# Running a filter's preparation in the unit that takes it, and three smaller reorderings, in a Fourier filter plus mixture-of-experts kernel

## The chip, the cores and the metric

The kernel runs on one core of one Trainium2 chip. The time is the device time of one execution in microseconds (us). Engines: PE (matmuls; PEld is its weight loads), DVE (vector), ACT (scalar), POOL (GpSimd), SP (issues nearly all DMAs). Each works through a queue of its own in order, and waits on semaphores.

## The reference, cut to what matters

```
xn  = layernorm(x)                                    # 2048 x 512
A   = irfft2(rfft2(xn) * (w_r + 1j * w_i))            # the filter
B   = sum over 8 experts e: gate_e(xn) * (gelu(xn @ w1[e]) @ w2[e])   # F = 1792, all experts kept
out = x + A + B
```

## The kernel before, in words

The experts' hidden columns are cut into 56 chunks of 256. Two are done in a front part (to about 133 us); the other 54 are taken in 27 pairs `c`, each for two halves `i` of the rows: 54 **units** `u = 2c + i`. `i = 0` is called a first half, `i = 1` a second half. Both layers of a unit are block products with fewer multiplications than the plain ones (Strassen-Winograd), so a unit has 7 products for layer 2 of the unit before and 7 for its own layer 1 (14 in all, 12 matmuls of 128x512 each). The PE order of a unit, by the tiles' names (weights `ua`, `us` and inputs `xr` for layer 1, `va`, `vs` and `hs` for layer 2; PSUM banks `A`, `B`, `C`):

`a11` to B, [layer 2] `s4` to C, `a12` to B, [layer 2] `s3` with input T3 to C, `s2` to A, [layer 2] `a11` to B, `s1` to A, [layer 2] `a12` to B, `s4` to A, [layer 2] `s1` with T1 to C, `s3` to B, [layer 2] `a22` with T4 to C, `a22` to B, [layer 2] `s2` with T2 to A.

The layer 2 products add up in place: after each, DVE adds the bank to the result (`acc<-C,acc`, `acc<-B,acc`, `acc<-A,acc`) before the next product may go on in that bank. The inputs of layer 2 are split in a rounded high part (ACT, `CAST hs<-c`) and the rest, the low part (DVE or POOL, `TENSOR_TENSOR hs<-c,hs`); a product reads the low part in its last four matmuls only.

`layer1` is a generator of 21 steps, `layer2` one of 7; the loop `for n in range(7)` at the end of `body` runs three steps of `layer1` (`one`) and one of `layer2` (`second`) per round, and puts the filter in between. The filter is a list of `chunks`, each a pair (PE part, DVE and ACT part, cost); `slot_pe()` issues the PE part of the next chunk and puts its other part into `todo`; `slot_dve()` issues what is in `todo`. All these are put in each engine's queue in the order of the code (`pin`); only the DMAs' places on SP are found when the program is built.

The filter has two kinds of chunks, for even and then odd frequencies. **Table chunks** (19 for each of four transforms; here "table" chunks have a PE part) issue 6 or 12 small matmuls into `psf` that need what the chunk before prepared: DVE `us<-us`, `B<-psf,B` or `C<-psf,C`, `uz<-us,uz` and ACT copies (line 438 is the filter's `op`). **Radix chunks** have no PE part: `radix4` (10 chunks of one `step` each, the last four half as large), `twiddle`, `multiply`, `combine`, `save`, `restore`; they are DVE operations on `Y` and the tiles `A` to `D`.

Before the change a unit takes table chunks in rounds 0, 2, 3 and 5, and radix chunks in rounds 0, 2, 3, 4 and, in first halves, 5. What was taken in round 5 is issued on DVE in round 0 of the next unit (`kept_back`), and what was then taken in round 0 only at the end of round 1.

Of the kernel before, what the change touches and what calls it, by code (L numbers as in the profile page):

```python
# [91 lines left out]
def r32(ap):  # L92
    return ap.bitcast(F32)
# [26 lines left out]
def body(ctx: ExitStack, tc: tile.TileContext, io):  # L120
    plain_order, strict, pinned = False, False, {}

    def pin(ins):
        if strict:
            engine = ins.ins.engine
            last = pinned.get(engine)
            if last is ins.ins:
                return ins
            if last is not None:
                tc.add_manual_dep(  # L130
                    ins.ins, last.name,
                    mybir.DependencyInfo(mybir.DependencyClass.NoSync, mybir.DependencyReason.DATA), reason="layout",
                )
            pinned[engine] = ins.ins
        return ins
# [51 lines left out]
    def load(src):  # L187
        raw = keep.tile([P, 8 * FC], F32, name="raw")
        nc.sync.dma_start(raw, src)
        return raw  # L190
# [46 lines left out]
    def move(dst, src):  # L237

        with tc.issue_after(last_sp[0]) if last_sp[0] else nullcontext():
            last_sp[0] = nc.sync.dma_start(dst, src).ins  # L240
# [185 lines left out]
    def filtered(p):  # L426
# [5 lines left out]
        out, of = [], {}  # L432

        def chunk(dve, cost, pe=None):
            out.append((pe, dve, cost))

        def op(fn, *args, **kw):
            return pin(fn(*args, **kw))  # L438
# [86 lines left out]
        def radix4(inner, sgn, first=None):  # L525

            def y(i):
                return of["Y"][:, i : i + 13 : 4] if inner else of["Y"][:, 4 * i : 4 * i + 4]

            def step(n):  # L530
                if n == 0 and first:
                    first()
                y0, y1, y2, y3 = (y(i) for i in range(4))
                t1, t3 = of["T1"], of["T3"]
                if n < 6:
                    add, d, a, b = (
                        (0, t1, y0, y2), (1, y0, y0, y2), (0, t3, y1, y3), (1, y1, y1, y3), (0, y2, y0, y1), (1, y0, y0, y1)
                    )[n]
                    op(V.tensor_add if add else V.tensor_sub, d, a, b)
                    return  # L540
                d, sg = ((y1, sgn), (y3, -sgn))[(n - 6) // 2]
                c = n % 2
                op(V.tensor_sub if (sg > 0) != c else V.tensor_add, d[:, :, c], t1[:, :, c], t3[:, :, 1 - c])

            for n in range(10):
                chunk(lambda n=n: step(n), 1.3 if n < 6 else 0.8)

        def twiddle(sgn):

# [45 lines left out]
        ends = slice(0, P + 1, P)  # L595

        def save():
            rev, w, z, ta, tb = (of["ends"][:, n] for n in range(5))
            op(V.tensor_add, w[:, :, 0], w[:, :, 0], rev[:, :, 0])
            op(V.tensor_sub, w[:, :, 1], w[:, :, 1], rev[:, :, 1])  # L600
            op(V.tensor_copy, z, of["Y"][:, :, :, ends])
            op(V.tensor_mul, ta, z, w[:, :, :1].to_broadcast([P, NB, 2, 2]))
            op(V.tensor_mul, tb, z, w[:, :, 1:].to_broadcast([P, NB, 2, 2]))

        def restore():
            rev, w, z, ta, tb = (of["ends"][:, n] for n in range(5))
            Y = of["Y"]
            op(V.tensor_sub, Y[:, :, 0, ends], ta[:, :, 0], tb[:, :, 1])
            op(V.tensor_add, Y[:, :, 1, ends], tb[:, :, 0], ta[:, :, 1])
            op(V.tensor_sub, Y[:, :, 0, :1], Y[:, :, 0, :1], Y[:, :, 1, P : P + 1])  # L610
            op(V.tensor_add, Y[:, :, 1, :1], Y[:, :, 1, :1], Y[:, :, 0, P : P + 1])

        if p == 0:
            chunk(save, 1.0)
        for j in range(8):
            chunk(lambda j=j: multiply(j), 1.4)
            chunk(lambda j=j: combine(j), 1.0)
        if p == 0:
            chunk(restore, 0.8)
        radix4(True, 1, narrow)  # L620
        twiddle(1)
        radix4(False, 1)
# [223 lines left out]
    chunks = deque()  # L846
# [7 lines left out]
    todo = []  # L854
# [18 lines left out]
    def slot_dve():  # L873

        while todo:
            todo.pop(0)()
# [83 lines left out]
    def xin(n, i):  # L960
        if (n, i) in ahead:
            return ahead.pop((n, i))
        x = xr.tile([P, 2, 2, TB], F32R, name="xr", bufs=3)
        last_x[0] = nc.sync.dma_start(r32(x), xs[n][i]).ins
        return x
# [333 lines left out]
    second, old, rs, spots = iter(()), [], {}, []  # L1299
    strict = True  # L1300
    for u in range(2 * N2):
        c, i = divmod(u, 2)
        if u and i == 0:
            raw = load(io["wb"][c])
            step2 = prepare(rp, "v", sums2(raw), w2q)
        if u == 1:
            ahead.update({(n, 1): xin(n, 1) for n in ("b11",)})
            behind = last_x[0]
            with tc.issue_after(behind):
                for b in range(NB - 4, NB):  # L1310
                    nc.sync.dma_start(res[b], acc[:, b, :])
            acc = keep.tile([P, 4, 2, 2, TB], F32, name="acc")
            ahead.update({(n, 1): xin(n, 1) for n in ("b21", "T1")})
            with tc.issue_after(last_x[0]):
                for n in ("T2", "T4"):
                    move(xs[n][1], r32(ahead[n, 1]))
        if i == 1 and c + 1 < N2:
            with tc.issue_after(behind) if u == 1 else nullcontext():
                raw = load(io["wa"][c + 1])
            step1 = prepare(wq, "u", sums1(raw, False), w1q)  # L1320
        hs = {}
        one = layer1(c, i, dict(w1q), hs, old)

        def weights(n):
            nonlocal strict
            strict = u > 0
            for _ in range(((3, 1, 1, 1, 1, 0, 0), (0, 0, 0, 2, 2, 2, 1), (0, 1, 1, 1, 2, 2, 1), (0, 1, 1, 1, 1, 2, 1))[min(u, 2 + i)][n]):
                with tc.issue_after(last_act[0]) if u == 0 else nullcontext():
                    next(step1 if i else step2, None)
            strict = True  # L1330

        end = u + 1 == 2 * N2
        if end:
            assert not chunks
            raw2 = raw[:, 2 * F2 : 3 * F2]
            nc.sync.dma_start(raw2, io["wb"][c][:, 2 * F2 : 3 * F2])
            y = ft.tile([P, NB, 2, P + 1], F32R, name="Y").rearrange("p a b c -> p (a b c)")
            both = [
                y[:, k * 4 * D : (k + 1) * 4 * D].rearrange("p (h k d) -> p h k d", h=2, k=2) for k in range(2)
            ]  # L1340
            ident = ft.tile([P, 2, 2, P], F32R, name="uz")
            ident = r32(ident.rearrange("p a b c -> p (a b c)"))[:, :P]
            nc.sync.dma_start(ident, idd)
            for n in "ABCD":
                y = wide(n)
                spots += [y[:, k * D : (k + 1) * D] for k in range(2)]
        for n in range(7):
            next(one)
            kept_back = bool(todo)
            if n == 0:  # L1350
                slot_dve()
            if u and not end and chunks:
                short = chunks[0][2] < 1.35 and not chunks[0][0]
                if n == 2 or n == 0 and u > 1 or n == 4 and short or n == 5 and (chunks[0][0] or i == 0 and short):
                    slot_pe()
            if n == 0 and not kept_back:
                slot_dve()
            if i:
                weights(n)
            if u == 1 and n == 0:  # L1360
                next(second)
            next(one)
            if u != 1 or n:
                next(second, None)
            if u and n == 3 and not end:
                slot_pe()
            if n in (2, 3, 4):
                slot_dve()
            next(one)
            if n == 1:  # L1370
                slot_dve()
            if not i:
                weights(n)
            if end:
                if n == 0:
                    finals(1)
                if n == 2:
                    split(both[0][:, :, :, FC:], raw2.rearrange("p (k f) -> p k f", k=2), nc.gpsimd)
                if 3 <= n < 6:
                    name = ("a11", "a12", "a22")[n - 3]  # L1380
                    dh, fh = (int(digit) - 1 for digit in name[1:])
                    pin(nc.scalar.copy(both[fh][:, :, :, dh * FC : (dh + 1) * FC], r32(w2q[name])))
                for b in ((), (), (12, 13), (14, 15), (4, 5), (6,), (7,))[n]:
                    rs[b] = rows_of(b, 1)
        second = layer2(c, i, w2q, hs)
# [53 lines left out]
```

## Time and profile before

| | us |
|---|---|
| median of 3 runs (lowest, highest) | 2479.45 (2474.74, 2481.25) |
| profiled execution | 2478.03 |
| its span, first to last instruction | 2476.2 |
| PE busy | 2342.3 (95%) |
| DVE busy | 1947.1 (79%) |
| POOL busy | 1411.9 (57%) |
| ACT busy | 1126.0 (45%) |

The profile is one execution. A row of the timeline gives start, duration, engine, line, operation, tiles, shapes and, in brackets, how long the engine had been idle and what ended that. L105 is the helper through which all main instructions go, L438 the filter's. Windows are given in us from the span's start; "PEclk" is the granted TensorE clock as a share of full speed. The units lie from 133.2 us (`u = 1`) to 2446 us; the table chunks fall in units 2 to 6, 22 to 31 and 48 to 52, the radix chunks in between.

### The profile page before, as it was taken

The page shows a single profiled execution, that of the slowest core. Times are in us where ns is not written, and L with a number is a line of the kernel's source. Part 1 is how long each engine was busy: PE and PEld are TensorE (multiplying, and loading weights), DVE is VectorE, ACT ScalarE, POOL GpSimd, SP SyncE. Part 2 cuts the span into 40 slices and gives each one's busy share as a digit, 9 for nine tenths or more (in the row PEclk, how much of TensorE's full clock was granted, in tenths as well). Part 3 has the DMA queues.
Part 4 walks back from the last instruction along what each step waited for, and adds up shares of the span by engine and source line. Part 5 has one row for each costly group of instructions (what it writes and reads, how often), then busy time and mean ns, then how long its engine had stood idle before and what let it go on. Part 6 is the DMA issues. An engine that isn't in the chain of part 4 may idle for free.

```text
span 2476.2 us, 27849 instructions
## 1 busy us (share of the span) xinstructions
PE 2342.3 (95%) x10478; PEld 1925.2 (78%) x10478; DVE 1947.1 (79%) x1753; ACT 1126.0 (45%) x1559; POOL 1411.9 (57%) x790
## 2 busy tenths in 40 slices
PE   9998889999999999998899889999999999989899
PEld 7777777778887778777787777778877787777777
DVE  8665666999889989867676667999889989866676
ACT  6554444454444454434344444454444454443342
POOL 3364445667666766654364445776666766653553
PEclk9999999999999999999999999999999999999999
DMA  7886756666677676767676556666666666766673
GB/s 255 321 310 220 235 198 230 238 237 239 240 258 268 213 280 219 263 240 257 225 246 221 200 215 212 236 228 240 230 246 211 247 219 232 266 236 240 235 258 139
DMA packets 123718, 588.58 MB, mean 238 GB/s; under 512 B 13600, under 2 KB 16288, under 8 KB 66880
## 3 DMA queue, kind: packets, MB, share of 16 engines
q1 hardware_dynamic: 122784, 574.06, 65.6%
q10 hardware_dynamic: 800, 12.74, 1.3%
q8 instruction: 83, 1.36, 0.2%
q14 instruction: 51, 0.42, 0.1%
HBM read 550.96 MB, written 48.37 MB: 242 GB/s over the span
## 4 chain that ended last, share of the span: by engine, by line
PE 77%; DVE 17%; ACT 2%; issue 2%; DMA 2%; POOL 0%; SPq 0%; ACTq 0%; DVEq 0%; POOLq 0%
PE B L105 31%; PE C L105 20%; PE A L105 19%; DVE c L105 7%; PE psf L438 5%; DVE acc L105 3%; DVE hs L105 2%; PE p L105 2%; DVE Y L438 2%; ACT hs L105 1%; DVE us L438 1%; PE psf L105 1%; DMA hs<-xs_T 1%; DVE uz L438 1%; DVE xr L105 1%
## 5 line engine op out<-in xcount | busy, mean ns | idle before, releaser
L105 POOL TENSOR_TENSOR hs<-c,hs 128x1024 fp32r<-128x1024 f32 x161 | 428.1, 2659 | 408.3 <-ACT hs L105 404.1
L105 ACT CAST hs<-c 128x1024 fp32r<-128x1024 f32 x375 | 390.4, 1051 | 217.6 <-DVE c L105 123.3
L105 PE MATMUL C<-hs,vs 128*128 128x512 f32 x1884 | 472.2, 401 | 8.7 <-DVE acc L105 8.7
L105 PE MATMUL A<-xr,us 128*128 128x512 f32 x1920 | 463.2, 390 | 0.0
L105 PE MATMUL B<-xr,ua 128*128 128x512 f32 x1884 | 455.5, 391 | 0.0
L105 PEld LDWEIGHTS C<-hs,vs 128*128 128x128 f32 x1884 | 365.2, 195 | 89.7 <-ACT ua L105 8.2
L105 PEld LDWEIGHTS A<-xr,us 128*128 128x128 f32 x1920 | 359.9, 188 | 74.8
L105 PEld LDWEIGHTS B<-xr,ua 128*128 128x128 f32 x1884 | 353.5, 188 | 76.3 <-DVE c L105 1.8
L105 DVE TENSOR_TENSOR hs<-c,hs 128x1024 fp32r<-128x1024 f32 x214 | 337.4, 1593 | 31.5 <-ACT hs L105 31.5
L105 DVE TENSOR_TENSOR c<-c 128x1024 f32<-128x1024 f32 x212 | 326.3, 1539 | 0.1
L105 PE MATMUL B<-hs,va 128*128 128x512 f32 x1248 | 312.3, 400 | 13.9 <-DVE acc L105 13.0
L105 DVE TENSOR_TENSOR acc<-C,acc 128x1024 f32<-128x1024 f32 x207 | 251.7, 1216 | 90.0 <-PE C L105 90.0
L105 PEld LDWEIGHTS B<-hs,va 128*128 128x128 f32 x1248 | 239.3, 194 | 70.2 <-DVE acc L105 17.2
L105 DVE TENSOR_TENSOR acc<-B,acc 128x1024 f32<-128x1024 f32 x103 | 125.7, 1220 | 156.0 <-PE B L105 156.0
L105 POOL TENSOR_TENSOR ua<-raw,ua 128x512 fp32r<-128x512 f32 x81 | 123.5, 1524 | 186.2 <-ACT ua L105 168.4
L105 ACT ACTIVATE c<-c 128x1024 f32<-128x1024 f32 x108 | 114.8, 1063 | 251.2 <-DVE c L105 251.2
L105 POOL TENSOR_TENSOR va<-raw,va 128x512 fp32r<-128x512 f32 x81 | 145.9, 1802 | 106.7 <-ACT va L105 106.7
L105 DVE TENSOR_TENSOR c<-c,cwb 128x1024 f32<-128x1024 f32 x108 | 196.8, 1822 | 1.5 <-ACT c L105 1.5
L105 ACT COPY c<-A 128x1024 f32<-128x1024 f32 x108 | 109.6, 1015 | 184.1 <-PE A L105 153.5
L105 DVE TENSOR_TENSOR c<-B,c 128x1024 f32<-128x1024 f32 x107 | 130.7, 1221 | 72.6 <-PE B L105 68.7
L105 PE MATMUL C<-hs,va 128*128 128x512 f32 x660 | 160.0, 391 | 0.2
L105 PE MATMUL B<-xr,us 128*128 128x512 f32 x636 | 153.4, 390 | 0.0
(188 smaller groups left out, 3071.6 us busy)
## 6 DMA issues: line engine op xcount, KB each, us to landing
xr<-xs_T SPq DMA_DIRECT2D x212, 1024.0 KB, 5.1
xr<-xs_b SPq DMA_DIRECT2D x161, 1024.0 KB, 5.1
cwb<-cwd SPq DMA_DIRECT2D x124, 256.0 KB, 5.0
raw<-in_wa SPq DMA_DIRECT2D x27, 1024.0 KB, 4.9
raw<-in_wb SPq DMA_DIRECT2D x27, 1024.0 KB, 4.9
xs_T<-Y SPq DMA_DIRECT2D x8, 1024.0 KB, 6.1
us<-xfd SPq DMA_DIRECT2D x32, 256.0 KB, 4.5
D<-mbd SPq DMA_DIRECT2D x32, 256.0 KB, 4.1
```

The source lines that it names most:

```text
L105: return lambda *args, **kw: self.order(made(*args, **kw))
L438: return pin(fn(*args, **kw))
```

## The change

1. A table chunk's DVE and ACT part is issued in the unit that took it: the one of round 5 in round 5, after the gate's multiplication of `h22`; the one of round 0 in round 0, after the low part of T3.
2. The fifth radix chunk of first halves is taken in round 1 and issued after T4's difference (`less(o12, o22, o21)`), not in round 5 and issued at the start of the second half.
3. Layer 2's first product and its `acc<-C,acc` come ahead of T3's low part on DVE.
4. The four half-size steps of each `radix4` become two chunks of two; `save` and `restore` become two chunks each. No operation is added or taken away; the filter has 14 chunks less (200, not 214).

```
-            for n in range(10):
-                chunk(lambda n=n: step(n), 1.3 if n < 6 else 0.8)
+            for n in range(6):
+                chunk(lambda n=n: step(n), 1.3)
+            for n in (6, 8):
+                chunk(lambda n=n: (step(n), step(n + 1)), 1.3)
...
         if p == 0:
-            chunk(save, 1.0)
+            chunk(save, 1.4)
+            chunk(save2, 1.4)
...
         if p == 0:
-            chunk(restore, 0.8)
+            chunk(restore, 1.4)
+            chunk(restore2, 1.3)
...
         for n in range(7):
             next(one)
-            kept_back = bool(todo)
-            if n == 0:
-                slot_dve()
             if u and not end and chunks:
-                short = chunks[0][2] < 1.35 and not chunks[0][0]
-                if n == 2 or n == 0 and u > 1 or n == 4 and short or n == 5 and (chunks[0][0] or i == 0 and short):
+                table = bool(chunks[0][0])
+                short = not table and chunks[0][2] < 1.35
+                if n == 2 or n == 0 and u > 1 or n == 4 and short or n == 5 and table or n == 1 and i == 0 and short:
                     slot_pe()
-            if n == 0 and not kept_back:
+            if n == 0 and todo and not table:
                 slot_dve()
             if i:
                 weights(n)
-            if u == 1 and n == 0:
-                next(second)
+            if n == 0:
+                next(second, None)
             next(one)
-            if u != 1 or n:
+            if n in (0, 5):
+                slot_dve()
+            if n:
                 next(second, None)
             if u and n == 3 and not end:
                 slot_pe()
             if n in (2, 3, 4):
                 slot_dve()
             next(one)
             if n == 1:
                 slot_dve()
```

**DVE at the seam of two table units** (end of `u = 3`, start of `u = 4`), from the gate's multiplication of `h22` on. `C<-psf,C` belongs to the chunk taken in round 5; `acc<-A,acc` ends the old unit's products, the last `hs<-c,hs` is T3's low part. Before:

```order
L105 TENSOR_TENSOR c<-c,cwb 128x1024
L105 TENSOR_TENSOR acc<-C,acc 128x1024
L105 TENSOR_TENSOR c<-B,c 128x1024
L105 TENSOR_TENSOR hs<-c,hs 128x1024
L105 TENSOR_TENSOR acc<-A,acc 128x1024
L105 TENSOR_TENSOR c<-c 128x1024
L438 TENSOR_TENSOR us<-us 128x256
L438 TENSOR_TENSOR C<-psf,C 128x260
L438 TENSOR_TENSOR uz<-us,uz 128x256
L105 TENSOR_TENSOR hs<-c,hs 128x1024
L105 TENSOR_TENSOR acc<-C,acc 128x1024
L105 TENSOR_TENSOR c<-c,cwb 128x1024
```

The same stretch now:

```order
L105 TENSOR_TENSOR c<-c,cwb 128x1024
L438 TENSOR_TENSOR us<-us 128x256
L438 TENSOR_TENSOR C<-psf,C 128x260
L438 TENSOR_TENSOR uz<-us,uz 128x256
L105 TENSOR_TENSOR acc<-C,acc 128x1024
L105 TENSOR_TENSOR c<-B,c 128x1024
L105 TENSOR_TENSOR hs<-c,hs 128x1024
L105 TENSOR_TENSOR acc<-A,acc 128x1024
L105 TENSOR_TENSOR c<-c 128x1024
L105 TENSOR_TENSOR acc<-C,acc 128x1024
L105 TENSOR_TENSOR hs<-c,hs 128x1024
L438 TENSOR_TENSOR us<-us 128x256
```

The three filter operations moved up by five operations; T3's low part stands behind `acc<-C,acc`; and the next chunk's `us<-us`, which stood behind T4's difference, six operations after T3's low part, follows that part at once.

**SP in a second half with table chunks** (`u = 5`), `xs_b_113` being the input of `a11` and `xs_T_115` that of `s2`. Before:

```order
L964 DMA xr<-xs_b_113 128x2048
L400 DMA cwb<-cwd 128x512 x2
L964 DMA xr<-xs_b_117 128x2048
L189 DMA raw<-in_wa 128x2048
L964 DMA xr<-xs_T_115 128x2048
L964 DMA xr<-xs_T_121 128x2048
L240 DMA us<-xfd_111 128x512
L240 DMA D<-mbd_200 128x512
```

Now:

```order
L974 DMA xr<-xs_b_113 128x2048
L400 DMA cwb<-cwd 128x512 x2
L974 DMA xr<-xs_b_117 128x2048
L240 DMA us<-xfd_111 128x512
L974 DMA xr<-xs_T_115 128x2048
L189 DMA raw<-in_wa 128x2048
L974 DMA xr<-xs_T_121 128x2048
L240 DMA D<-mbd_200 128x512
```

The filter's load into `us` stands ahead of the load for `s2` and of the weights (`raw`); it stood behind both.

**DVE in a first half with radix chunks**, from the third product's `acc<-C,acc` on; `c<-c` is T4's difference. Before (`u = 10`):

```order
L105 TENSOR_TENSOR acc<-C,acc 128x1024
L105 TENSOR_TENSOR c<-c 128x1024
L105 TENSOR_TENSOR acc<-B,acc 128x1024
L438 TENSOR_TENSOR B<-Y 128x8x129
L105 TENSOR_TENSOR hs<-c,hs 128x1024 x2
```

Now, in a first half a little further on:

```order
L105 TENSOR_TENSOR acc<-C,acc 128x1024
L105 TENSOR_TENSOR c<-c 128x1024
L438 TENSOR_TENSOR Y<-Y 128x4x258
L105 TENSOR_TENSOR acc<-B,acc 128x1024
L438 TENSOR_TENSOR Y<-Y 128x4x258
L105 TENSOR_TENSOR hs<-c,hs 128x1024 x2
```

A filter step stands between T4's difference and `acc<-B,acc`, where there was none; in second halves the step ahead of `acc<-B,acc` is gone in exchange.

More of the change, by code (lines that the diff above doesn't have):

```diff
@@ L600, in save, with save2 @@
             op(V.tensor_sub, w[:, :, 1], w[:, :, 1], rev[:, :, 1])
+        def save2():
+            rev, w, z, ta, tb = (of["ends"][:, n] for n in range(5))
             op(V.tensor_copy, z, of["Y"][:, :, :, ends])
@@ L609, in restore, with restore2 @@
             op(V.tensor_add, Y[:, :, 1, ends], tb[:, :, 0], ta[:, :, 1])
+        def restore2():
+            Y = of["Y"]
             op(V.tensor_sub, Y[:, :, 0, :1], Y[:, :, 0, :1], Y[:, :, 1, P : P + 1])
```

## The prediction

> **What bounds the kernel now.** I read the page first, then PE's waits, then the stages as windows, then single units in the timeline. The page and the list of what PE waited for:
>
> ```profile
> PE 2342.3 (95%) x10478; PEld 1925.2 (78%) x10478; DVE 1947.1 (79%) x1753; ACT 1126.0 (45%) x1559; POOL 1411.9 (57%) x790
> ...
> PE psf L438 <- DVE uz L438: 53.6, 17, 3.4
> PE psf L438 <- DVE us L438: 30.1, 9, 3.8
> PE psf L438 <- issue: 14.6, 7, 2.4
> PE B L105 <- DVE acc L105: 13.0, 10, 1.7
> PE C L105 <- DVE acc L105: 8.7, 10, 2.4
> ```
>
> PE sets the time, and nearly all it waits for is DVE: 98.3 us in 33 waits ahead of the filter's matmuls, 21.7 us in 20 waits until an addition had freed bank B or C. Where these lie, and what they cost with what follows them, is read from the windows (length, then PE, PEld, DVE, ACT and POOL busy, granted clock, DMA share, GB/s): table units 2 to 6, radix 7 to 21, table 22 to 31, radix 32 to 47, table 48 to 52, and last two single units, 9 and 10.
>
> ```profile
> 179.50:436.90 257.40, 229.36 (x1033) 190.56 (x1031) 161.62 (x152) 115.99 (x190) 119.41 (x69) 0.95 0.63 218
> 436.90:1024.90 588.00, 577.60 (x2521) 472.30 (x2521) 536.49 (x410) 278.38 (x353) 403.68 (x212) 1.00 0.68 244
> 1024.90:1525.60 500.70, 452.56 (x2065) 377.00 (x2064) 331.96 (x324) 212.00 (x322) 237.79 (x140) 0.96 0.66 229
> 1525.60:2152.70 627.10, 616.32 (x2690) 505.34 (x2689) 570.11 (x426) 295.27 (x374) 425.71 (x224) 1.00 0.67 236
> 2152.70:2403.40 250.70, 225.70 (x1033) 187.73 (x1032) 166.40 (x169) 98.66 (x137) 115.91 (x70) 0.96 0.71 245
> 515.40:555.80 40.40, 38.66 (x169) 31.41 (x168) 39.29 (x30) 20.33 (x33) 28.77 (x15) 1.00 0.72 261
> 555.80:594.00 38.20, 38.20 (x169) 31.41 (x167) 34.47 (x25) 16.72 (x21) 23.14 (x13) 1.00 0.66 234
> ```
>
> Unit 10 has PE busy for all its 38.2 us: 14 products of 2.73. That is the floor of a unit. Line 438's own rows in the three table stages, and one undisturbed group in the timeline, give the floor with the filter:
>
> ```profile
> 179.50:436.90 257.40, 32.54 (x192) 29.70 (x192) 33.35 (x50) 27.18 (x80) 0.95 0.63 218
> 1024.90:1525.60 500.70, 61.83 (x384) 57.37 (x384) 61.06 (x114) 37.54 (x111) 0.96 0.66 229
> 2152.70:2403.40 250.70, 30.42 (x192) 27.95 (x192) 27.30 (x64) 10.95 (x32) 0.96 0.71 245
> ...
> 277.44 0.88 PE L438 MATMUL psf<-B,D 128*128 128x260 f32 x6
> 278.16 2.94 PE L105 MATMUL C<-hs,va 128*128 128x512 f32 x12
> ```
>
> Table stages: 20 units in 1008.8 us; the floor is 20 x 38.2 + 128 groups of six at 0.72 = 764.0 + 92.2, so 152.6 us too much. Radix stages: 31 units in 1215.1 us against 1184.2, so 30.9 too much, and, from unit 9 against 10, in second halves: there DVE is busy 39.3 of 40.4 us.
>
> **The table chunks' preparation (152.6 us).** PE and DVE around the seam into unit 4:
>
> ```profile
> 286.39 2.88 PE L105 MATMUL B<-xr,ua 128*128 128x512 f32 x12
> 292.64 0.99 PE L438 MATMUL psf<-A,uz 128*128 128x260 f32 x6 [3.36 <-DVE uz L438]
> 308.37 1.64 PE L438 MATMUL psf<-A,uz 128*128 128x260 f32 x6 [3.07 <-DVE uz L438]
> ...
> 289.07 0.41 DVE L438 TENSOR_TENSOR us<-us 128x256 f32<-128x256 f32 x1
> 291.58 0.43 DVE L438 TENSOR_TENSOR C<-psf,C 128x260 fp32r<-128x260 f32 x1 [2.10 <-ACT C L438]
> 292.16 0.43 DVE L438 TENSOR_TENSOR uz<-us,uz 128x256 fp32r<-128x256 f32 x1
> 292.50 1.22 DVE L105 TENSOR_TENSOR hs<-c,hs 128x1024 fp32r<-128x1024 f32 x1
> ...
> 307.08 1.15 DVE L438 TENSOR_TENSOR uz<-us,uz 128x256 fp32r<-128x256 f32 x1
> ```
>
> Twice a unit PE reaches a group (rounds 0 and 2) whose `uz` DVE writes only then: the piece was held back to just after the seam, or behind T4's difference. The new order, walked with these durations (1.2 us for a full-size operation such as T3's low part at 292.50, 0.4 for a filter piece, 2.73 for a product): the round 5 group follows `s3`; four products (10.9 us) lie between it and the group of round 0. Behind `s3` DVE does the sum into `h22`, a difference, and, once ACT's gelu is done, a multiplication: about 3.8 us; then three pieces, 1.2 us. They end 4.9 us after `s3`, and are wanted at 1.4 + 10.9 = 12.3: 7.4 us in hand, against 3.36 short. Round 0, from the start of `a11`: product 2.7, group 1.4, `s4` to 6.9, `acc<-C` to 8.1, T3's low part to 9.3, pieces to 10.5; the group of round 2 stands at 6.9 + 3 x 2.73 = 15.1: 4.6 us in hand, against 3.07 short. Both waits go, and nothing in between holds PE: the T3 product starts at 9.6 (C is free at 8.1) and wants the low part eight matmuls later, at 11.4.
>
> The change adds one wait: ACT's copy of `uz` awaits `us<-us`, now about 9.7 us into the unit, and T1's high part and the gelu of bank B queue behind it; a12 ends only at 9.6, so the gelu is some 2 us late, done at about 12.7. POOL's order is the same as before; it sees T1's high part that much later, and needs it for a product three rounds on.
>
> What is late next is bank B: its `c<-B,cwb` now comes behind the filter's pieces, two operations and the gelu, at about 14.5, and layer 2's product wants B at 16.5. With 2 us in hand an undisturbed unit doesn't wait; where POOL delays DVE by one operation (about 2 us, below) it waits a few tenths. Bounds: nothing, and 2.2 us a unit (unit 9's excess, with a wait of 1.74). I take 0.45 x 20 = 9 us, nearer to nothing, since DVE, busy 161.6 us in the five units of the first table stage, or 32 a unit, keeps some 11 of 44 us free. Gain 152.6 - 9 = 143.6.
>
> How much of that is the waits themselves? They sum to 98.3 us; the granted clock of 0.95, 0.96 and 0.96 costs 12.9 + 20.0 + 10.0 = 42.9 us more. This stretch follows the wait of 3.07:
>
> ```profile
> 310.00:313.40 3.40, 3.40 (x17) 3.04 (x16) 0.00 (x0) 1.06 (x3) 0.00 (x0) 0.81 0.46 177
> ```
>
> No radix stage shows less than 1.00, so I count the low clock to the waits. [...]
>
> **The radix step and the freed C (30.9 us).** A second half (unit 9), then one with `multiply` (unit 15):
>
> ```profile
> 532.38 2.95 DVE L438 SCALAR_TENSOR_TENSOR Y<-Y,C 128x258 f32<-128x258 f32 x2
> 535.25 1.21 DVE L105 TENSOR_TENSOR acc<-B,acc 128x1024 f32<-128x1024 f32 x1
> 536.52 3.06 PE L105 MATMUL B<-hs,va 128*128 128x512 f32 x12 [1.74 <-DVE acc L105]
> ...
> 754.43 3.42 DVE L105 TENSOR_TENSOR hs<-c,hs 128x1024 fp32r<-128x1024 f32 x1
> 757.77 1.21 DVE L105 TENSOR_TENSOR acc<-C,acc 128x1024 f32<-128x1024 f32 x1
> 759.13 2.99 PE L105 MATMUL C<-hs,vs 128*128 128x512 f32 x12 [2.36 <-DVE acc L105]
> ```
>
> In unit 9 a filter step of 2.95 us stands ahead of `acc<-B`; without it the bank is free 2.9 us earlier, more than the 1.74. In unit 15 the order of the two operations costs 2.36; reversed, C is free 3.3 us earlier. Second halves thus keep four steps of five and lose both waits.
>
> First halves get the fifth step and the exchange. Unit 10:
>
> ```profile
> 560.73 1.23 DVE L105 TENSOR_TENSOR hs<-c,hs 128x1024 fp32r<-128x1024 f32 x1 [1.02 <-ACT hs L105]
> 572.38 1.22 DVE L105 TENSOR_TENSOR acc<-B,acc 128x1024 f32<-128x1024 f32 x1 [2.37 <-PE B L105]
> 579.17 3.28 DVE L438 TENSOR_TENSOR Y<-Y 128x1032 f32<-128x1032 f32 x1
> 584.65 1.32 DVE L438 TENSOR_TENSOR Y<-Y 128x1032 f32<-128x1032 f32 x1
> 578.97 2.40 POOL L105 TENSOR_TENSOR hs<-c,hs 128x1024 fp32r<-128x1024 f32 x1 [3.07 <-ACT hs L105]
> ```
>
> The exchange costs DVE 0.6 us: `acc<-C` must await 5.5 us into the unit, where T3's low part started at 4.9. The step costs 1.32 undisturbed, 3.28 beside POOL. Ahead of it DVE has 2.37 us idle before `acc<-B`, which may itself end 1.5 us later (a product of 2.73 lies between), in all 3.9; 0.6 + 3.28 just fits. I take 1.32 to 2.3, and for residual waits in first halves and the few beside `multiply` 4.5 us together, between 0 and the 30.9 that second halves pay today for the same overload. Gain 26.4. [...]
>
> Half steps joined two by two, and `save` and `restore` cut: the same operations, so nothing of their own; a unit's four or five steps are now all of full size, which the 4.5 us includes. The filter ends about three units sooner; nothing waits for that end.
>
> **DMAs.** Each table chunk brings along a load into `us` and one of a table, now issued in the round that took it. In SP's queue the `us` load stands ahead of an input's load and can't start before DVE has read the tile. The page's rows:
>
> ```profile
> xr<-xs_T SPq DMA_DIRECT2D x212, 1024.0 KB, 5.1
> us<-xfd SPq DMA_DIRECT2D x32, 256.0 KB, 4.5
> ```
>
> Three `xr` buffers let an input's load start when the third product before it ends, some 13.7 us (five products) ahead of use, so 8.5 us are in hand; the `us` load of round 5 frees SP at 4.9 us after `s3`, while the input behind it can start at 4.2 anyway. Cost 0.7 of 8.5: nothing. A unit of 44 us instead of 54 carries the same bytes: a DMA share of 0.63 to 0.71 becomes about 0.8.
>
> **Sum.** 2478.03 (the profiled execution, 1.4 below the median) - 143.6 - 26.4 = 2308; on the median's footing 2309.
>
> **Rivals.**
> - First halves overload: each fifth step blocks as its 3.28 row, and some 15 first halves wait 2.2 us as second halves do now, less the 4.5 already counted. For: unit 10 has 2.37 us idle and no more. Against: few POOL operations lie there. 2309 + 28 = 2337.
> - Bank B late in table units, 2.2 us in each of 20, less the 9 counted: 2309 + 35 = 2344; with the overload 2372.
> [...]
> - One of the two table waits stays, held by the load of `us` and not by the order: half of 152.6 back, 2385. Against: DVE waited for ACT or nothing there, not for a DMA.
> - Slower: SP. If a `us` load held the queue over 8.5 us, PE would wait for inputs; from about 8.5 + 8.5 us (170 us of gain over 20 units) in each table unit it decides. It would be so if the load's tile came free only with the next chunk, some 17 us on: about 2500. Against: the tile is read by the chunk's own first pieces.
>
> **How the numbers follow.** Forecast (2293 to 2326) 0.68; overload 0.11; bank B, alone or with it, 0.08; clock 0.04; one wait stays 0.05; SP 0.03; no difference 0.01. The range goes from all 183.5 us gone and 3 us of scatter (2291) to 2368, which takes in the first two rivals and leaves out some 0.15. Within 0.3% (7 us) is about what can't be told from no change: faster 0.95, same 0.02, slower 0.03.
>
> **What would show it.** Table units of 44 to 45 us, none of the `psf` waits on DVE, a granted clock near 1.00 everywhere, second halves at 38.2. I am wrong if table units show a new wait on B or C over 1 us, if first halves rise above 38.5, or if PE waits for `xr`.

## The result and the profile after

| | us |
|---|---|
| median before, in the same session (4 runs) | 2479.98 |
| median after (4 runs, 2323.37 to 2325.18) | 2323.85 |
| ratio, 95% interval | 0.9375 [0.9359, 0.9391] |
| profiled execution after, its span | 2323.53, 2321.7 |

156 us are gone; 2309 was forecast. The page's engine row, and what PE still waits for (waits for whom: us in total, times, longest):

```profile
PE 2296.7 (99%) x10478; PEld 1891.6 (81%) x10478; DVE 1960.1 (84%) x1753; ACT 1128.1 (49%) x1559; POOL 1429.1 (62%) x790
...
PE B L105 <- DVE c L105: 12.1, 24, 1.7
PE B L105 <- DVE acc L105: 1.9, 4, 0.6
PE C L105 <- DVE acc L105: 1.6, 4, 0.4
PE B L105 <- ACT acc L105: 1.5, 1, 1.5
```

All waits of the filter's `psf` groups have left the list, and those on `acc` fell from 21.7 to 3.5 us. One wait has grown: bank B on DVE `c`, 24 times, 12.1 us, where it was one wait of 0.9 us. The windows by stage, as before: table units 2 to 6, radix 7 to 20, table 21 to 30, radix 31 to 43, table 44 to 48, and four units 49 to 52 that now have no filter left.

```profile
179.80:395.20 215.40, 214.91 (x1033) 180.75 (x1033) 165.01 (x151) 116.62 (x189) 126.77 (x69) 1.00 0.73 261
395.20:941.30 546.10, 541.01 (x2354) 440.73 (x2354) 517.06 (x391) 260.68 (x332) 374.97 (x198) 1.00 0.70 248
941.30:1371.20 429.90, 429.13 (x2066) 360.99 (x2064) 337.63 (x326) 211.39 (x322) 250.98 (x141) 1.00 0.74 266
1371.20:1880.70 509.50, 502.68 (x2185) 409.07 (x2185) 481.81 (x361) 243.36 (x312) 352.03 (x184) 1.00 0.67 235
1880.70:2094.90 214.20, 214.20 (x1034) 180.72 (x1033) 161.02 (x168) 98.76 (x136) 118.37 (x70) 1.00 0.81 290
2094.90:2248.70 153.80, 153.46 (x674) 126.21 (x673) 116.81 (x85) 72.13 (x84) 98.50 (x57) 1.00 0.67 234
```

By the prediction's floor (38.2 a unit, 0.72 a group of six), the 20 table units take 859.5 us against 764.0 + 92.2: 3.3 too much, where it was 152.6. The 27 radix units take 1055.6 against 1031.4: 24.2 too much, where 31 units had 30.9. The clock is 1.00 in every stage.

The seam into unit 4, which was shown before:

```profile
267.99 3.02 PE L105 MATMUL B<-xr,ua 128*128 128x512 f32 x12 [0.49 <-DVE c L105]
270.85 0.88 PE L438 MATMUL psf<-A,uz 128*128 128x260 f32 x6
283.20 0.88 PE L438 MATMUL psf<-A,uz 128*128 128x260 f32 x6
...
262.71 1.51 DVE L438 TENSOR_TENSOR us<-us 128x256 f32<-128x256 f32 x1
264.49 1.18 DVE L438 TENSOR_TENSOR uz<-us,uz 128x256 fp32r<-128x256 f32 x1
266.73 1.21 DVE L105 TENSOR_TENSOR c<-B,c 128x1024 f32<-128x1024 f32 x1
...
275.21 1.23 DVE L105 TENSOR_TENSOR acc<-C,acc 128x1024 f32<-128x1024 f32 x1 [3.22 <-PE C L105]
278.16 0.42 DVE L438 TENSOR_TENSOR uz<-us,uz 128x256 fp32r<-128x256 f32 x1
280.90 1.23 DVE L105 TENSOR_TENSOR c<-B,cwb 128x1024 f32<-128x1024 f32 x1
```

Neither `psf` group shows a wait. The `uz` of round 5 is done at 265.7 and wanted at 270.85; that of round 0 at 278.6, wanted at 283.20: 5.2 and 4.6 us in hand. The one wait left here, 0.49, is `a11` of unit 4 waiting for the last reading of bank B (`c<-B,c`, 266.73), which the pieces, 1.51 and 1.18 instead of 0.42, push back.

### The profile page after: what moved, and what is told of

The parts are those of the page before. It is cut to its first block, busy times and chain, and to the rows that moved or that the text cites. A ratio compares the mean times of both kernels' runs of the same rounds, so it can differ in the third digit from the quotient of the medians.

```text
span 2321.7 us, 27882 instructions
## 1 busy us (share of the span) xinstructions
PE 2296.7 (99%) x10478; PEld 1891.6 (81%) x10478; DVE 1960.1 (84%) x1753; ACT 1128.1 (49%) x1559; POOL 1429.1 (62%) x790
## 4 chain that ended last, share of the span: by engine, by line
PE 73%; DVE 23%; issue 2%; DMA 1%; ACT 1%; POOL 0%; DVEq 0%; ACTq 0%; POOLq 0%
PE B L105 29%; PE C L105 19%; PE A L105 18%; DVE c L105 9%; DVE hs L105 5%; PE psf L438 4%; DVE Y L438 4%; DVE acc L105 3%; PE p L105 2%; PE psf L105 1%; DVE xr L105 1%; DMA xs_T<-Y 0%; DMA us<-xfd 0%; DVE us L438 0%; DVE uz L438 0%
## 5 line engine op out<-in xcount | busy, mean ns | idle before, releaser
L105 POOL TENSOR_TENSOR hs<-c,hs 128x1024 fp32r<-128x1024 f32 x161 | 404.9, 2516 | 402.4 <-ACT hs L105 396.0
L105 PE MATMUL C<-hs,vs 128*128 128x512 f32 x1884 | 456.1, 390 | 0.4
L105 PEld LDWEIGHTS C<-hs,vs 128*128 128x128 f32 x1884 | 352.5, 188 | 75.2 <-DVE hs L105 2.4
L105 DVE TENSOR_TENSOR hs<-c,hs 128x1024 fp32r<-128x1024 f32 x214 | 372.9, 1761 | 6.1 <-ACT hs L105 6.1
L105 DVE TENSOR_TENSOR c<-c 128x1024 f32<-128x1024 f32 x212 | 345.8, 1631 | 0.1
L105 PE MATMUL B<-hs,va 128*128 128x512 f32 x1248 | 304.9, 393 | 8.6 <-DVE c L105 6.4
L105 PEld LDWEIGHTS B<-hs,va 128*128 128x128 f32 x1248 | 231.4, 188 | 66.8 <-DVE c L105 14.1
L105 POOL TENSOR_TENSOR ua<-raw,ua 128x512 fp32r<-128x512 f32 x81 | 137.5, 1698 | 134.8 <-ACT ua L105 111.7
L105 DVE TENSOR_TENSOR acc<-B,acc 128x1024 f32<-128x1024 f32 x103 | 125.3, 1217 | 41.0 <-PE B L105 40.9
L105 DVE TENSOR_TENSOR c<-c,cwb 128x1024 f32<-128x1024 f32 x108 | 155.4, 1439 | 2.2 <-ACT c L105 2.2
```

The source lines that it names most:

```text
L105: return lambda *args, **kw: self.order(made(*args, **kw))
```

## The experiments

The median of the kernel before was 2478.86 to 2479.98 us in the four sessions; its single runs scatter by up to 10 us, so the intervals of kernels only 7 us apart overlap. The runs of those kernels themselves don't (after 2323.4 to 2325.2, undo_c_first 2315.4 to 2318.1, undo_joined_steps 2315.7 to 2317.8), but they come from different sessions, and no effect is read from differences of 2 us or less.

| kernel | parts | median us | ratio to before, 95% interval |
|---|---|---|---|
| after | 1 2 3 4 | 2323.85 | 0.9375 [0.9359, 0.9391] |
| only_table | 1 | 2335.33 | 0.9426 [0.9409, 0.9442] |
| undo_c_first | 1 2 4 | 2316.09 | 0.9349 [0.9332, 0.9366] |
| undo_joined_steps | 1 2 3 | 2317.25 | 0.9352 [0.9335, 0.9368] |
| undo_radix_place | 1 3 4 | 2338.36 | 0.9439 [0.9422, 0.9456] |
| hold_round5 | 1 in half, 2 3 4 | 2421.14 | 0.9768 [0.9755, 0.9782] |
| hold_round0 | 1 in half, 2 3 4 | 2391.45 | 0.9646 [0.9633, 0.9659] |
| c_first_in_table_units | 1 2 4, 3 in table units | 2312.03 | 0.9328 [0.9315, 0.9341] |
| c_first_table_and_single_steps | 1 2, 3 in table units | 2302.14 | 0.9288 [0.9276, 0.9301] |
| table_and_radix_place | 1 2 | 2311.56 | 0.9321 [0.9308, 0.9334] |
| c_first_alone | 3 | 2481.34 | 1.001 [1.0, 1.002] |

**only_table.** The loop before, with a table chunk's part issued in rounds 0 and 5:

```
+            if n == 0 and not kept_back and not table:
                 slot_dve()
...
             next(one)
+            if table and n in (0, 5):
+                slot_dve()
```

> The kernel before with part 1 alone (table chunks' preparation issued in its own unit; radix chunks, operand order and chunk list as before). Theory: the two psf waits of a table unit and the low clock behind them were the 152 us, so table units fall to 44 us and the second halves' 30 us stay: 2480 - 150 = 2330, granted clock 1.00 in table stages. Rival: part of the 152 us came back in new waits that parts 2 to 4 then removed: over 2345. Second rival: parts 2 to 4 cost more than they bring: below 2324.

Measured 2335.3. Part 1 alone is worth 143.5 us of the 156. Its first table stage and first radix stage:

```profile
180.10:395.30 215.20, 215.12 (x1033) 180.84 (x1033) 161.62 (x150) 116.45 (x189) 125.26 (x69) 1.00 0.74 261
395.30:944.70 549.40, 540.26 (x2354) 442.02 (x2353) 496.93 (x384) 258.94 (x331) 371.27 (x197) 1.00 0.68 244
```

The table stage is 1.2 us above its floor (5 x 38.2 + 32 x 0.72 = 214.0 us) and its clock at 1.00; the second halves' waits stay, 549.4 us for 14 units against 534.8. A wait of 0.67 us for bank C appears in seven units of the inverse transforms, which take 44.9 us where the changed kernel's take 44.0: some 6 us together, about the 5 by which the time is over the expected one. It is short of the first rival's 2345.

**hold_round5 and hold_round0.** The changed kernel with one of the two table pieces held back again:

```
+            if n == 0:                     # hold_round5, ahead of slot_pe
+                slot_dve()
...
-            if n in (0, 5):
+            if n == 0:
                 slot_dve()
...
-            if n in (0, 5):                # hold_round0
+            if n == 5:
                 slot_dve()
```

> The changed kernel, but the table piece taken in round 5 is again issued at the start of the next unit. Theory: the wait of 2.8 to 3.8 us at the seam returns in 17 or 18 units with the low clock behind it, the wait of round 2 does not: 2324 + 75 = about 2400, granted clock 0.96 to 0.98 in table stages. [...]

> The changed kernel, but the table piece taken in round 0 is again issued at the end of round 1, behind T4's difference. Theory: the wait of round 2 (1.6 to 3.1 us) returns in 16 units with the low clock where it is long: 2324 + 55 to 75 = about 2390. Rival (it is short because the seam's wait ahead of it is gone, and DVE is early): under 2360.

2421.1 and 2391.5: 97 and 68 us, together 165 us, against the 149 that both were worth in these stages (152.6 - 3.3); either wait returns by itself. hold_round5 cost 20 us more than expected. PE's waits in it, and below them those of hold_round0:

```profile
PE psf L438 <- DVE uz L438: 31.4, 10, 3.4
PE psf L438 <- DVE us L438: 28.3, 8, 3.8
PE psf L438 <- ACT Y L438: 5.2, 2, 2.6
...
PE psf L438 <- DVE uz L438: 25.9, 8, 3.7
PE psf L438 <- issue: 12.9, 6, 2.6
PE psf L438 <- DVE us L438: 5.3, 2, 3.2
```

The 64.9 us of waits in hold_round5 cost 97 us, with a clock of 0.984 over the span against 1.00. After which waits these traces show the low clock is told in the last section.

**undo_c_first, undo_joined_steps, undo_radix_place.** Each takes one of the parts 2 to 4 back, as in the lines of the diff above with the minus sign (for part 2, together with `kept_back`; part 1 stays).

> The changed kernel with part 3 undone (T3's low part ahead of layer 2's first product and its addition again). Theory, from the trace after: behind the addition T3's low part starts 0.7 to 1.8 us later and meets POOL, which costs 0.46 us in some 17 second halves and part of the 11 us in first halves, against about 2.4 us in the 4 or 5 second halves that have a multiply chunk in round 0: 2324 - 3, so 2316 to 2326. Rival (the exchange removes all of the waits on C, 8.7 us with what follows): 2333 or more.

> The changed kernel with part 4 undone (ten radix chunks with four half-size ones, save and restore whole). Theory: two half steps in one slot beside POOL cost 3.7 us and make the sum into h22 late in units 8, 10, 18, 32 and 34 (1.2 to 1.9 us each); apart they fit: about 2317. Rival (same operations, no effect): 2324. Second rival (more chunks, so more full slots elsewhere): over 2326.

> The changed kernel with part 2 undone (fifth radix chunk of first halves taken in round 5 and issued at the next unit's start, that unit's round 0 chunk behind T4's difference). Theory: second halves wait for bank B again, about 2.0 us in some 10 of them (20 us), and first halves lose their 11 us: about 2333. Rival (the overload was only moved from second to first halves and moves back at no price): 2322 to 2326.

2316.1, 2317.3 and 2338.4. Without part 3 the kernel is 7.8 us faster, without part 4 6.6 us; without part 2 it is 14.5 us slower. So part 2 pays, and 3 and 4, as built, cost. The first came out at the edge of what was expected, the third 5 us slower: with part 2 taken back, but parts 3 and 4 kept, a second half that gets its fifth step back waits up to 2.3 us for bank B. The mechanism of part 3 shows in unit 49, a second half without any filter. It starts at 2094.90 in the changed kernel and at 2088.68 in undo_c_first, whose rows stand below the dots:

```profile
2100.56 1.23 DVE L105 TENSOR_TENSOR acc<-C,acc 128x1024 f32<-128x1024 f32 x1 [2.72 <-PE C L105]
2101.70 2.60 DVE L105 TENSOR_TENSOR hs<-c,hs 128x1024 fp32r<-128x1024 f32 x1
2105.36 2.32 DVE L105 TENSOR_TENSOR c<-c 128x1024 f32<-128x1024 f32 x1
2107.61 1.21 DVE L105 TENSOR_TENSOR c<-B,cwb 128x1024 f32<-128x1024 f32 x1
2100.81 2.41 POOL L105 TENSOR_TENSOR hs<-c,hs 128x1024 fp32r<-128x1024 f32 x1 [1.82 <-ACT hs L105]
2104.90 1.70 POOL L105 TENSOR_TENSOR ua<-raw,ua 128x512 fp32r<-128x512 f32 x1 [1.68 <-ACT ua L105]
2108.87 1.43 PE L105 MATMUL B<-hs,va 128*128 128x512 f32 x5 [0.17 <-DVE c L105]
...
2093.60 1.23 DVE L105 TENSOR_TENSOR hs<-c,hs 128x1024 fp32r<-128x1024 f32 x1 [1.98 <-ACT hs L105]
2095.88 2.29 DVE L105 TENSOR_TENSOR c<-c,cwb 128x1024 f32<-128x1024 f32 x1
2098.10 1.21 DVE L105 TENSOR_TENSOR c<-c 128x1024 f32<-128x1024 f32 x1
2099.23 1.21 DVE L105 TENSOR_TENSOR c<-B,cwb 128x1024 f32<-128x1024 f32 x1
2094.60 2.49 POOL L105 TENSOR_TENSOR hs<-c,hs 128x1024 fp32r<-128x1024 f32 x1 [1.82 <-ACT hs L105]
```

In the changed kernel DVE sits idle 2.72 us for bank C; in the last 0.7 of these T3's low part could already run. The last reading of bank B (`c<-B,cwb`) then starts 12.7 us into the unit, against 10.6 without part 3, and PE waits for the bank (0.17 us, with 0.46 us lost in the unit, 38.68 instead of 38.22). One DVE operation runs long beside POOL's own `hs` in both kernels: T3's low part in the first (2.60 instead of 1.23), `c<-c,cwb` in the second (2.29 instead of 1.22), so that meeting makes a difference of only 0.3 us. Of the 2.2 us by which the reading is late, 0.7 are this idle time, and 1.1 are `c<-c`, which comes so late that it runs beside POOL's next operation as well (2.32 instead of 1.21). In unit 10 of the changed kernel part 4 shows:

```profile
537.78 3.63 DVE L438 TENSOR_TENSOR Y<-A,B 128x516 f32<-128x516 f32 x2
543.60 3.25 DVE L438 TENSOR_TENSOR Y<-A,B 128x516 f32<-128x516 f32 x2
546.77 1.21 DVE L105 TENSOR_TENSOR c<-B,c 128x1024 f32<-128x1024 f32 x1
548.03 2.35 PE L105 MATMUL B<-xr,ua 128*128 128x512 f32 x9 [1.25 <-DVE c L105]
```

Two pairs of half steps, 6.9 us, stand ahead of the sum into `h22`, which frees bank B 1.25 us late for the next product.

**c_first_in_table_units, c_first_table_and_single_steps.** If part 3 helps table units alone, it should be there alone:

```
-            if n == 0:
+            first = n == 0 and (u == 1 or u > 1 and not end and bool(chunks) and table)
+            if first:
                 next(second, None)
             next(one)
             if n in (0, 5):
                 slot_dve()
-            if n:
+            if not first:
                 next(second, None)
```

The second of the two also has part 4 undone.

> The changed kernel with the addition ahead of T3's low part in table units only, radix units as before. Theory: the exchange is worth 0.9 us in 7 units of the inverse transforms (they wait 0.67 us for C without it) and costs some 13 us in radix units; so the undone exchange's 2316.1 less 6: about 2310. Rival (the waits on C in the inverse units only move to B): 2316.

> The same, and the half steps, save and restore as before the change (part 4 undone as well). Theory: both savings add up, some 13 us by the exchange and 6.6 by single steps: 2304 to 2308. Rival (single steps take more slots, which fill second halves that the exchange had relieved): 2310 or more.

2312.0 and 2302.1. The savings add up and a little more (11.8 and 6.6 us one by one, 21.7 together, so the second came out 2 us below its range), and the second is the fastest kernel here. What PE waits for in it:

```profile
PE B L105 <- DVE c L105: 3.3, 5, 1.1
PE B L105 <- ACT acc L105: 1.5, 1, 1.5
PE psf L105 <- POOL xr masks.py:199: 1.4, 1, 1.4
PE p L105 <- DVE xr L105: 1.2, 1, 1.2
PE C L105 <- DVE acc L105: 1.0, 4, 0.5
```

**table_and_radix_place, c_first_alone.** Parts 1 and 2 alone, and part 3 alone on the kernel before.

> Parts 1 and 2 alone (parts 3 and 4 undone). Theory: the radix chunk's new place is by itself worth the 26 us that the prediction gave to parts 2 to 4 together, and 3 and 4 gave some of it back: 2335 - 26 = 2309, with the 0.9 us waits on C in 7 inverse table units left. Rival (the place needs part 3, since second halves with a multiply chunk wait 2.4 us for C): 2316 or more.

> The kernel before with part 3 alone. Theory: it removes the waits on C (2.4 us in 3 or 4 second halves, 11 us with what follows), and costs second halves, whose DVE is full, up to 0.5 us each (14 of them): 2472 to 2484, that is no difference. Rival (it is what makes second halves wait for B, by delaying the queue behind it): 2490 or more.

2311.6: with part 1 in place, part 2 by itself is worth 23.8 us (2335.3 to 2311.6), and 3 and 4 on top of both cost 12.3. Part 3 alone makes no difference above 0.3% (2481.3, 0.0 to 0.2% slower): it took the waits on C away, and put others on B. In c_first_alone, PE's waits on the banks read

```profile
PE B L105 <- DVE c L105: 11.5, 18, 1.7
PE B L105 <- DVE acc L105: 9.2, 12, 1.1
```

where it had 13.0 on B (DVE `acc`), 0.9 on B (DVE `c`) and 8.7 on C before. So part 3 makes waits on `c` without any of the other parts. In the changed kernel about half of them are its doing: 12.1 us fall to 6.1 in undo_c_first, and most of what stays lies at seams of table units and in units with joined steps.

## Why the prediction was right, and where a size was off

- *The table chunks' preparation.* Right, in place and size: 152.6 us fell to 3.3 (9 were left to it). Of the 98.3 us of waits put down to DVE, the list gives 14.6 (7 waits) to "issue"; they are gone too, and hold_round0 brings 12.9 us of them back, so they hung on the held piece as well. The walk of round 0 held: 275.21 for `acc<-C` is 7.2 us into the unit (6.9 worked out), `uz` 10.6 (10.5), the group of round 2 15.2 (15.1), `c<-B,cwb` done at 14.1 (14.5). For the piece of round 5 the walk was 2.2 us too generous (7.4 us in hand against 5.2), since it took pieces at 0.4 us that ran at 1.51 and 1.18. The wait named as next, bank B late behind the pieces, came at the seam instead, 1.06, 0.49 and 0.70 us ahead of units 3, 4 and 26; the first is over the 1 us that the prediction named as a sign of being wrong. That only_table gained 143.5 us against the 143.6 forecast is partly luck: its residual lay in waits for bank C, not in the 9 us set aside for bank B. only_table, hold_round5 and hold_round0 show that both pieces are needed.
- *The low clock goes with the waits.* Right: 1.00 in every stage after, and low again where one wait was put back (0.984 and 0.992 over the spans of hold_round5 and hold_round0). Its argument, that no radix stage shows less than 1.00, holds to two decimals only: behind unit 41's wait of 2.35 us the kernel before has a low stretch too (0.50 from 1888.25 to 1891.66 us), and that unit takes 42.5 us where units 15 and 39 take 40.9 with the same wait. That it would stay low without them, to which 0.04 went, is out.
- *The radix step.* Right in kind: part 2 by itself brings 23.8 us (table_and_radix_place). But the 26.4 us were forecast for parts 2 to 4 together, and these brought 11.5 (only_table to the changed kernel), for the two reasons that follow.
- *The freed C: mis-sized.* "The exchange costs DVE 0.6 us" was read from unit 10, where T3's low part waited for ACT anyway, and it was set against first halves alone. The first delay is of that size (0.7 us in unit 49). What was left out is that an operation behind it then runs beside another one of POOL's (`c<-c` in unit 49, 2.32 us instead of 1.21), which makes 2.2 us there, in second halves above all, which had been counted as cured: ten of them take 38.7 us. It costs 7.8 us in the changed kernel, net of what it brings in table units.
- *Joined half steps: mis-sized.* "The same operations, so nothing of their own": they are the same, but two in one slot ahead of one bank's release are late where one was not. 6.6 us.
- The residual of the radix stages, put at 4.5 us, is therefore 24.2, and the 5.7 us that the table term came out better don't make it up: 2309 + 20 - 6 = 2323.
- *First halves overload* (the first rival) came in part: units 8, 10, 32 and 34 take about 40 us, over the 38.5 that the prediction named as a sign of being wrong, yet through the joined steps and the exchange; with single steps and the exchange in table units only, PE's waits on B and C for DVE are 4.3 us in all.
- *DMAs.* Right: PE waits for no `xr` load, and the DMA share in table stages is 0.73, 0.74 and 0.81 where 0.8 was worked out (from one unit of 54 us; the stages' mean was 50.4). The SP rival didn't happen.

## What to carry to other kernels

Work that an engine prepares for the next use should go into its queue as soon as its inputs exist; held to a seam it cost two waits a unit and a lower clock behind them, about 150 us. An operation that must wait for another engine doesn't belong ahead of one that is ready, unless the wait is what frees the resource in time: judge it unit by unit, as here table units gained by it and the others lost. When operations are joined, look at who waits behind the pair, not only at their sum.

## What the runs showed of the hardware beyond that

In the trace of the kernel before the low clock lies on a grid of 3.41 us: it goes low, to 0.50, 28 times, from 185.00 to 2475.34 us, each time a whole number of steps of 3.413 us behind the first (to within 0.02 us), for 3.41 us (once 6.83, from 1069.05; the last time to the end). The length of a wait alone doesn't tell whether it does. Stretches of hold_round5 on a grid of the same step, with a wait of 3.37 us in unit 3 and one of 3.37 in unit 5 (PE busy is the first number after the length, the granted clock the third from the end):

```profile
229.47:232.88 3.41, 1.34 (x6) 0.76 (x5) 3.07 (x3) 2.03 (x3) 2.79 (x2) 1.00 0.57 151
232.88:236.29 3.41, 2.12 (x10) 2.12 (x11) 0.85 (x2) 1.79 (x6) 0.00 (x0) 0.50 1.00 423
328.46:331.87 3.41, 1.72 (x8) 1.10 (x6) 2.80 (x3) 1.65 (x2) 2.52 (x2) 1.00 0.56 192
331.87:335.28 3.41, 1.73 (x13) 1.73 (x14) 0.85 (x2) 2.17 (x7) 0.00 (x0) 1.00 1.01 425
335.28:338.69 3.41, 3.41 (x16) 2.77 (x16) 0.63 (x1) 0.68 (x2) 0.00 (x0) 1.00 1.00 406
```

Where one stretch holds 2.07 us of the wait, the next is granted 0.50; where the grid cuts the same wait in 1.69 and 1.68, nothing follows. Laid on the traces of before, after, only_table and the two held-back kernels, the clock goes low 60 times: 58 times after a stretch in which PE was idle for at least 1.86 us (the other two lie at the end of the span), and, the first 10 us apart, no stretch with over 1.95 us idle is followed by a full clock; in the kernel before alone it is 27 times after 1.90 us or more, and 1.94 us is the most that a full clock follows. Eight times, the one shown among them, it stays low for a second stretch; in each of these PE was idle for 0.81 us or more of the first, and in none of the other low stretches within the span for more than 0.49. So in these runs a wait of 2 us can already cost another 1.7 (an estimate, half of 3.41; unit 41's 42.5 us are 1.6 above the 40.9 of units 15 and 39), and the one of 3.37 in unit 5 cost none. In hold_round5 a clock of 0.984 over 2422 us is worth up to 39 us (an estimate), which with the 64.9 us of waits covers the 97.

The low clock is not bound to the table stages. In only_table unit 15 has the wait for bank C that the prediction shows in the kernel before (2.36 us, the product behind it 2.99 us long):

```profile
717.47 4.58 PE L105 MATMUL C<-hs,vs 128*128 128x512 f32 x12 [2.35 <-DVE acc L105]
```

Before, the grid cut this wait at 758.37 us in 1.60 and 0.76, and the clock stayed at 1.00. Here the product behind it takes 4.58 us, as in unit 41 of the kernel before (4.57), where the whole 2.35 us lie in the stretch from 1884.84 us and the next is granted 0.50; the unit takes 42.5 us, against 40.9 before, for the same wait.
